# All sums of expert weights on VectorE, row weighting on ScalarE, and one copy ahead of a relu: gated linear attention feeding a mixture of experts

## The chip, the cores and the metric

The kernel runs on one core of a Trainium2 chip. The metric is device time in microseconds (us), median of several executions. One more execution is recorded by the hardware profiler; every row below comes from that one. Engines are named as in the profile: PE is TensorE's matmul side, PEld its weight loads, DVE is VectorE, ACT is ScalarE, POOL is GpSimd, SP is SyncE. A trailing q (PEq, ACTq) is that engine's sequencer.

## The reference, cut to what matters

Attention (4 batches, 8 heads, 768 steps, head size 48) gives 3072 tokens of 384 numbers. Each token then goes to one of 16 experts (4 groups of 4), whose result is scaled by the two gate weights:

```python
for g in range(G):
    xg = x[g_idx == g]
    ...
    for e in range(Eg):
        h = np.maximum(xg[mask_e] @ w1[g, e], 0.0)       # 384 -> 1024
        ye = h @ w2[g, e]                                # 1024 -> 384
        combined = g_w[mask_g][mask_e] * e_w[mask_e]
        out[tok_idx] = combined[:, None] * ye
```

All of it is float32.

## The kernel before, in words

Until about 128 us the attention runs and the tokens are sorted into slots by expert; the change touches nothing there. From then on experts are worked off one after the other, as "jobs". Job 0 is a small early piece, jobs 1 to 15 go through the function `seven`, and a last small job ends the kernel. Job j has 2m tokens (m falls from 108 to 84). The order of instructions on each engine is the order in which the program issues them; each engine works its own queue in order.

`seven` computes both layers with seven block products instead of eight, so it needs sums of weight blocks (s1 to s4, for each layer) and sums of token blocks (t1 to t5). On PE, one call of `add` or `sum_of` is a group of 16 matmul instructions. This text numbers them. First layer: G1 (a11 b11), G2 (a12 b21), G3 (a13 b31), G4 (s2 t2), G5 (s1 t1), G6 (s3 t3), G7 (a23 b32), G8 (s4 b22), G9 (a13 b32), G10 (a22 t4), G11 (a23 t5). Second layer: H1 (a11 c11), H2 (a12 c21), Z (32 instructions, the last third of the outputs), H3 (s2 t2), H4 (s1 t1), H5 (s3 t3), H6 (s4 c22), H7 (a22 t4). Each PSUM sum is built up over several groups, and partial sums are copied out between them by ACT: k1 after G1 (L1254), k2 after G4 (L1260), k5 after G5 (L1262), k3 after G7 (L1266). The same bank goes on being added to, so G6 has to wait until k2 is copied, G8 until k5 is, and G10 until k3 is.

DVE adds the copies up into the four quarters of the hidden layer: c11 (L1258), c22 (L1268), c12 (L1272); ACT puts the relu on each (L1239) and on c21, which comes straight from the bank of G11. Then DVE makes the token sums of the second layer (L1208 to L1211), turns the rows of the next job into columns (`columns`, L1342), makes its token sums (again L1208 to L1211, L1219), and adds up parts of the result (L1304, L1313, L1315). The last part of the result is an ACT copy (L1317).

The weight sums of one layer are four instructions on 128x512 numbers: s1, s2 on DVE (L1188, L1189) and s3, s4 on POOL (L1192, L1193). `work_between` says where in `seven` they are issued. In the kernel before, those of the next job's first layer are all issued at "third" (ahead of L1313 on DVE); those of its second layer on DVE at "fourth" (ahead of the destinations L1352, L1360 of that job) and on POOL at its "first".

The results of job j-1 are delivered at "first" of job j: DVE transposes them (L1327), DVE multiplies them with the tokens' weights (L1330), and POOL issues 6 or 7 indirect DMAs (L1334) that scatter the rows to the output. At "second", from job 2 on, one step of a small table for left-over tokens is made on DVE (`table_of_left_overs`, ten steps of different lengths).

Of the kernel before, what the change touches and what calls it, by code (L numbers as in the profile page):

```python
# [17 lines left out]
ALU = mybir.AluOpType  # L18
AF = mybir.ActivationFunctionType
# [4 lines left out]
P = 128  # L24
# [86 lines left out]
def gla_then_hierarchical_moe(  # L111
# [32 lines left out]
    nc = tc.nc  # L144
# [7 lines left out]
    DM = H * D  # L152
# [24 lines left out]
    QW = DM // 4 + 2  # L177
# [10 lines left out]
    def bank():  # L188
        return banks["of"].tile([P, 512], F32, name="bank")
# [991 lines left out]
    def weight_sums(a, first):  # L1181

        ws = mp.tile([P, 4, 512], F32, name="ws_1" if first else "ws_2")
        s1, s2, s3, s4 = (ws[:, i] if first else
                          ws[:, i].rearrange("p (f d) -> p f d", f=4) for i in range(4))

        def by_vector():
            nc.vector.tensor_tensor(out=s1, in0=a(1, 0), in1=a(1, 1), op=ALU.add)  # L1188
            nc.vector.tensor_tensor(out=s2, in0=s1, in1=a(0, 0), op=ALU.subtract)  # L1189

        def by_pool():
            nc.gpsimd.tensor_tensor(out=s3, in0=a(0, 0), in1=a(1, 0), op=ALU.subtract)  # L1192
            nc.gpsimd.tensor_tensor(out=s4, in0=a(0, 1), in1=s2, op=ALU.subtract)  # L1193

        return dict(of=(s1, s2, s3, s4), by_vector=by_vector, by_pool=by_pool)

    def first_sums(j):
        w1 = weights[j][0]
# [24 lines left out]
    def seven(job, w1, w2, xt, sums, tokens, between):  # L1223


        m = job["n"] // 2
        n = 2 * m
        V, A = nc.vector, nc.scalar
        hT = mp.tile([P, FC, CAP], F32, name="hT")
        quarter_of = [hT[:, 4 * i:4 * i + 4, k * m:k * m + m] for i in range(2) for k in range(2)]  # L1230
        c11, c12, c21, c22 = quarter_of
        kept = mp.tile([P, 4, 4, CAP // 2], F32, name="kept", bufs=1)
        k1, k2, k3, k5 = (kept[:, i, :, 0:m] for i in range(4))

        def four(z):
            return z[:, 0:4 * m].rearrange("p (f t) -> p f t", f=4)

        def relu_of(c, z=None):
            A.activation(out=c, in_=c if z is None else z, func=AF.Relu)  # L1239

        def add(z, w, x, start=False):
            for f in range(4):
                onto(z[:, f * m:(f + 1) * m], w[:, f * P:(f + 1) * P], x, start and f == 0)

        b11, b12, b21, b22 = (xt[:, dc, k * m:(k + 1) * m] for dc in range(2) for k in range(2))
        b31, b32 = (xt[:, 2, k * m:(k + 1) * m] for k in range(2))
        a11, a12, a13, a21, a22, a23 = (w1[:, dc, i * 512:(i + 1) * 512]
                                        for i in range(2) for dc in range(3))
        s1, s2, s3, s4 = sums[0]["of"]
        t1, t2, t3, t4, t5 = tokens  # L1250
        za, zb, zc = bank(), bank(), bank()

        add(za, a11, b11, True)
        A.copy(out=k1, in_=four(za))  # L1254
        add(zb, a12, b21, True)
        add(zb, a13, b31)
        between("first")
        V.tensor_tensor(out=c11, in0=k1, in1=four(zb), op=ALU.add)  # L1258
        add(za, s2, t2)
        A.copy(out=k2, in_=four(za))  # L1260
        add(zc, s1, t1, True)
        A.copy(out=k5, in_=four(zc))  # L1262
        add(za, s3, t3)
        add(za, a23, b32)
        relu_of(c11)
        A.copy(out=k3, in_=four(za))  # L1266
        between("second")
        V.tensor_tensor(out=c22, in0=k3, in1=k5, op=ALU.add)  # L1268
        add(zc, s4, b22)
        add(zc, a13, b32)  # L1270
        relu_of(c22)
        V.tensor_tensor(out=c12, in0=k2, in1=four(zc), op=ALU.add)  # L1272
        add(za, a22, t4)
        add(za, a23, t5)
        relu_of(c12)
        relu_of(c21, four(za))

        ts = mp.tile([P, 4, 4, CAP // 2], F32, name="ts_2", bufs=1)
        t1, t2, t3, t4 = (ts[:, i, :, 0:m] for i in range(4))
        token_sums(*quarter_of, t1, t2, t3, t4)  # L1280
        a11, a12, a21, a22 = (w2[:, 4 * k:4 * k + 4, i * P:(i + 1) * P]
                              for i in range(2) for k in range(2))
        s1, s2, s3, s4 = sums[1]["of"]
        yT = results[0]
        results.reverse()
        last = mp.tile([P, 4, CAP // 2], F32, name="kept_y", bufs=1)
        k1, k2, k3, k5 = (last[:, i, 0:m] for i in range(4))
        za, zb, zc, zd = (bank()[:, 0:w] for w in (m, m, m, n))

        def sum_of(z, w, x, start=False):  # L1290
            for f in range(4):
                onto(z, w[:, f], x[:, f], start and f == 0)

        sum_of(za, a11, c11, True)
        A.copy(out=k1, in_=za)
        sum_of(zb, a12, c21, True)
        between("weights")
        for f in range(FC):
            w = w2[:, f, 2 * P:3 * P]
            if job.get("whole"):  # L1300
                product(zd, w, hT[:, f, 0:n], n, f == 0, f == FC - 1)
            else:
                onto(zd, w, hT[:, f, 0:n], f == 0)
        V.tensor_tensor(out=yT[:, 0, 0:m], in0=k1, in1=zb, op=ALU.add)  # L1304
        between("third")
        A.copy(out=yT[:, 2, 0:n], in_=zd)
        sum_of(za, s2, t2)
        A.copy(out=k2, in_=za)
        sum_of(zc, s1, t1, True)
        A.copy(out=k5, in_=zc)  # L1310
        sum_of(za, s3, t3)
        A.copy(out=k3, in_=za)  # L1312
        V.tensor_tensor(out=yT[:, 1, m:n], in0=k3, in1=k5, op=ALU.add)  # L1313
        sum_of(zc, s4, c22)
        V.tensor_tensor(out=yT[:, 0, m:n], in0=k2, in1=zc, op=ALU.add)  # L1315
        sum_of(za, a22, t4)
        A.copy(out=yT[:, 1, 0:m], in_=za)  # L1317
        between("fourth")
        return yT
# [3 lines left out]
    def deliver_quarters(job, yT, dst):  # L1323

        nb, rows = job["nb"], job["rows"]
        yq = mp.tile([P, NB, DM // 4], F32, name="yq")
        nc.vector.transpose(  # L1327
            out=yq[:, 0:nb].rearrange("p b (c r) -> p b c r", c=DC),
            in_=yT[:, :, 0:32 * nb].rearrange("p c (b t) -> p b c t", t=32))
        nc.vector.tensor_tensor(  # L1330
            out=yq[:, 0:nb], in0=yq[:, 0:nb],
            in1=rows[:, 0:nb, QW - 2:QW - 1].to_broadcast([P, nb, DM // 4]), op=ALU.mult)
        for b in range(nb):
            nc.gpsimd.indirect_dma_start(  # L1334
                out=out_by.popleft().rearrange("n (j w) -> (n j) w", j=4),
                out_offset=bass.IndirectOffsetOnAxis(ap=dst[:, b:b + 1], axis=0),
                in_=yq[:, b, :], in_offset=None, bounds_check=4 * N - 1, oob_is_err=False)
# [131 lines left out]
    def deliver_last():  # L1469
        deliver_quarters(*pending.popleft())  # L1470
# [58 lines left out]
    xt = ahead["xt"]  # L1529
    sums = {1: [first_sums(1), second_sums(1)]}  # L1530
    tokens = {1: first_tokens(xt, ahead["n"] // 2)}
    for part in sums[1]:
        part["by_vector"]()
        part["by_pool"]()
    left_overs = table_of_left_overs()
    end = len(jobs) - 1
    turned = {1: xt}

    def work_between(j, what):
        job, after = jobs[j], jobs[j + 1]  # L1540
        if what == "first":
            if j > 1:
                sums[j][1]["by_pool"]()
            deliver_last()
        elif what == "second":
            if 1 < j:
                next(left_overs, None)
        elif what == "weights":
            if j + 2 < len(jobs):
                load_w1(j + 2, expert(jobs[j + 2]))  # L1550
        elif what == "third":
            if j == end - 1:
                n_left = nc.values_load(
                    table["n_more"][0:1, 0:1], min_val=0, max_val=NX,
                    skip_runtime_bounds_check_because="a count of at most NX")
                computed_left_over(n_left)
            turned[j + 1] = columns(after)
            if j + 1 < end:
                tokens[j + 1] = first_tokens(turned[j + 1], after["n"] // 2)
                sums[j + 1] = [first_sums(j + 1), second_sums(j + 1)]  # L1560
                sums[j + 1][0]["by_vector"]()
                sums[j + 1][0]["by_pool"]()
        elif what == "fourth":
            if j + 2 < len(jobs):
                load_w2(j + 2, expert(jobs[j + 2]))
            if j + 1 < end:
                sums[j + 1][1]["by_vector"]()

    jobs[end - 1]["whole"] = True
    for j, job in enumerate(jobs):  # L1570
        if j == 0:
# [84 lines left out]
```

## Time and profile before

| what | value |
|---|---|
| median of 3 runs | 420.25 us (415.59 to 421.2) |
| profiled execution, own time | 415.17 us |
| its span, first to last instruction | 413.2 us |
| mean granted TensorE clock | 0.977 |
| ACT busy in the span | 156.8 us |
| POOL busy in the span | 291.5 us |

The span is 2.0 us shorter than the execution's own time; steps below are made in the span and carried over one to one. The median lies 5.1 us above the profiled execution.

### The profile page before, as it was taken

How to read it: one execution, taken by the hardware profiler on the slowest of the kernel's cores; microseconds unless marked ns; L12 is line 12 of the kernel's file. 1: busy time of each engine (PE TensorE's matmuls, PEld its weight loads, DVE VectorE, ACT ScalarE, POOL GpSimd, SP SyncE). 2: the span in 40 equal slices, each digit the busy share in tenths (PEclk: the TensorE clock that was granted, in tenths of full speed). 3: DMA queues.
4: the chain of work that ended last, by engine and by line, in shares of the span. 5: the costliest groups of instructions: out<-in, count | busy, mean ns of one | idle time of the engine just before them, and what ended most of it. 6: DMA issues, size and time to landing. Idle time of an engine off the chain costs nothing. (4 is left out here: it accounts for less than half of the span.)

```text
span 413.2 us, 16779 instructions
## 1 busy us (share of the span) xinstructions
PE 369.2 (89%) x7098; PEld 339.5 (82%) x7098; DVE 335.3 (81%) x625; ACT 156.8 (38%) x430; POOL 291.5 (71%) x300
## 2 busy tenths in 40 slices
PE   7999999989899899898998888896998979779795
PEld 5888888868798798897988877796988979779794
DVE  7696999979677897887898789988889889788620
ACT  2767756755632223423232332323132332333220
POOL 7899599899764548585766767685766857667544
PEclk9999999999999999998999899997899999999898
DMA  8999998889868985666676555664677578547200
GB/s 299 393 398 376 390 372 275 291 276 367 300 239 255 235 302 194 199 221 182 233 250 221 184 186 183 189 221 156 203 264 251 184 214 295 199 172 245 101 24 31
DMA packets 32859, 98.87 MB, mean 239 GB/s; under 512 B 17957, under 2 KB 22179, under 8 KB 28432
## 3 DMA queue, kind: packets, MB, share of 16 engines
q1 hardware_dynamic: 26896, 87.14, 61.5%
q0 software_dynamic: 4832, 9.55, 6.6%
q8 instruction: 57, 0.93, 0.9%
q10 hardware_dynamic: 1056, 1.10, 0.9%
q14 instruction: 18, 0.15, 0.1%
HBM read 82.61 MB, written 15.60 MB: 238 GB/s over the span
## 5 line engine op out<-in xcount | busy, mean ns | idle before, releaser
L1334 POOL DMA_INDIRECT out_dram<-yq,dst_q x101 | 110.3, 1092 | 59.4 <-issue 26.1
L1178 PE MATMUL bank<-ts,ws 128*64 128x108 f32 (+14 forms) x1440 | 68.7, 248 | 1.0 <-PEq L1503 0.6
L1178 PE MATMUL bank<-hT,w 128*64 128x108 f32 (+28 forms) x928 | 65.9, 302 | 2.0 <-ACT hT L1239 2.0
L1178 PEld LDWEIGHTS bank<-ts,ws 128*64 128x64 f32 x1440 | 63.8, 137 | 4.3 <-issue 3.4
L1193 POOL TENSOR_TENSOR ws<-w,ws 128x512 f32<-128x512 f32 x30 | 38.9, 1296 | 35.6 <-DVE ws L1189 35.6
L1178 PE MATMUL bank<-ts,w 128*64 128x108 f32 (+14 forms) x720 | 39.3, 263 | 26.9 <-ACT kept L1266 26.9
L1178 PEld LDWEIGHTS bank<-hT,w 128*64 128x64 f32 x928 | 56.4, 149 | 7.9 <-ACT hT L1239 2.2
L1178 PEld LDWEIGHTS bank<-ts,w 128*64 128x64 f32 x720 | 34.4, 147 | 29.7 <-ACT kept L1266 29.7
L1178 PE MATMUL bank<-xt_e,w 128*64 128x106 f32 (+13 forms) x1120 | 54.8, 246 | 1.8 <-issue 1.8
L1178 PEld LDWEIGHTS bank<-xt_e,w 128*64 128x64 f32 x1120 | 50.0, 137 | 2.1 <-issue 1.9
L1313 DVE TENSOR_TENSOR yT<-kept_y 128x108 f32<-128x108 f32 (+14 forms) x15 | 38.9, 2593 | 12.4 <-ACT kept_y L1312 11.5
L1239 ACT ACTIVATE hT<-hT 128x432 f32<-128x432 f32 (+14 forms) x45 | 22.9, 529 | 62.1 <-DVE hT L1258 50.3
L1192 POOL TENSOR_TENSOR ws<-w 128x512 f32<-128x512 f32 x30 | 40.5, 1351 | 2.0 <-DMA slots_d<-xr,place 1.9
L459 DVE TENSOR_TENSOR_SCAN kd<-in,starts 112x516 f32<-112x516 f32 (+1 forms) x21 | 24.3, 1162 | 7.1 <-DMA in<-in_rows_dram 7.1
L736 POOL DMA_INDIRECT slots_d<-xr,place x24 | 24.1, 1004 | 6.3 <-issue 3.9
L475 POOL TENSOR_TENSOR in<-in,kd 112x512 f32<-112x512 f32 (+1 forms) x21 | 23.9, 1139 | 5.4 <-DVE kd L459 3.5
L582 PE MATMUL bank<-wr,yt 112*64 112x116 f32 x384 | 25.4, 267 | 1.5 <-ACT yt L574 1.5
L493 PE MATMUL zs<-in 48*64 48x128 f32 (+1 forms) x512 | 22.8, 276 | 3.6 <-POOL in L479 3.4
L479 POOL TENSOR_TENSOR in<-in,cq 112x512 f32<-112x512 f32 (+1 forms) x22 | 23.9, 1093 | 2.8 <-DVE cq L470 2.7
L470 DVE TENSOR_TENSOR_SCAN cq<-in,starts 112x516 f32<-112x516 f32 (+1 forms) x22 | 24.6, 1127 | 1.4
L1189 DVE TENSOR_TENSOR ws<-ws,w 128x512 f32<-128x512 f32 x30 | 24.6, 820 | 1.0
L1188 DVE TENSOR_TENSOR ws<-w 128x512 f32<-128x512 f32 x30 | 24.9, 829 | 0.0
(207 smaller groups left out, 689.2 us busy)
## 6 DMA issues: line engine op xcount, KB each, us to landing
w<-in_w_dram SPq DMA_DIRECT2D x34, 1536.0 KB, 7.3
in<-in_rows_dram SPq DMA_DIRECT2D x17, 962.5 KB, 10.0
slots_d<-blank SPq DMA_DIRECT2D x4, 1372.0 KB, 18.9
w<-in_rows_dram SPq DMA_DIRECT2D x4, 962.5 KB
xq<-slots_d SPq DMA_DIRECT2D x28, 85.8 KB, 5.7
xq<-slots_d SPq DMA_DIRECT2D x28, 73.5 KB, 6.3
out_dram<-yq,dst_q POOLq DMA_INDIRECT x101
in<-in_rows_dram SPq DMA_DIRECT2D x1, 704.0 KB
```

The source lines that it names most:

```text
L459: nc.vector.tensor_tensor_scan(out=flat(c.kd[:, p0:p1])[:, ::-1], data0=c.t[0:R, A1 * p1:A1 * p0:-1], data1=one_col.to_broadcast([R, A1 * ...
L470: nc.vector.tensor_tensor_scan(out=flat(c.cq[:, p0:p1]), data0=c.t[0:R, A1 * p0:A1 * p1], data1=starts[0:R, A1 * p0:A1 * p1], initial=1.0, ...
L475: nc.gpsimd.tensor_tensor(out=c.k[:, p0:p1], in0=c.k[:, p0:p1], in1=c.kd[:, p0:p1, 1:A1], op=ALU.mult)
L582: nc.tensor.matmul(z[s, p * W:(p + 1) * W], lhsT=c.yt[:, p, s], rhs=wr[:, p, :], start=True, stop=True)
L736: sent = nc.gpsimd.indirect_dma_start(out=slots_by[t], out_offset=bass.IndirectOffsetOnAxis(ap=m["place"][:, c:c + 1], axis=0), in_=xr[:, ...
L1178: nc.tensor.matmul(z[h], lhsT=w[:, h], rhs=x, start=start, stop=False, skip_group_check=True)
L1188: nc.vector.tensor_tensor(out=s1, in0=a(1, 0), in1=a(1, 1), op=ALU.add)
L1189: nc.vector.tensor_tensor(out=s2, in0=s1, in1=a(0, 0), op=ALU.subtract)
L1192: nc.gpsimd.tensor_tensor(out=s3, in0=a(0, 0), in1=a(1, 0), op=ALU.subtract)
L1193: nc.gpsimd.tensor_tensor(out=s4, in0=a(0, 1), in1=s2, op=ALU.subtract)
L1313: V.tensor_tensor(out=yT[:, 1, m:n], in0=k3, in1=k5, op=ALU.add)
L1334: nc.gpsimd.indirect_dma_start(out=out_by.popleft().rearrange("n (j w) -> (n j) w", j=4), out_offset=bass.IndirectOffsetOnAxis(ap=dst[:, b ...
```

## The change

The multiplication of the delivered rows goes from one DVE instruction to one ACT instruction for each of the 6 or 7 row blocks. s3 and s4 go from POOL to DVE, and POOL is left with the indirect DMAs alone. The places of issue change: at "third" only s1, s2 of the next job's first layer are issued; s3, s4 of it stand at "first", behind the transpose of the delivered rows and ahead of c11; all four sums of the second layer stand behind c11 at a new place, "sums", together with the step of the left-over table. Nothing of this is issued at "fourth" any more. The copy k3 is issued ahead of the relu of c11 instead of behind it.

```diff
-        def by_vector():
+        def two():
             nc.vector.tensor_tensor(out=s1, in0=a(1, 0), in1=a(1, 1), op=ALU.add)
             nc.vector.tensor_tensor(out=s2, in0=s1, in1=a(0, 0), op=ALU.subtract)
 
-        def by_pool():
-            nc.gpsimd.tensor_tensor(out=s3, in0=a(0, 0), in1=a(1, 0), op=ALU.subtract)
-            nc.gpsimd.tensor_tensor(out=s4, in0=a(0, 1), in1=s2, op=ALU.subtract)
-
-        return dict(of=(s1, s2, s3, s4), by_vector=by_vector, by_pool=by_pool)
+        def other_two():
+            nc.vector.tensor_tensor(out=s3, in0=a(0, 0), in1=a(1, 0), op=ALU.subtract)
+            nc.vector.tensor_tensor(out=s4, in0=a(0, 1), in1=s2, op=ALU.subtract)
+
+        return dict(of=(s1, s2, s3, s4), two=two, other_two=other_two)
...
         between("first")
         V.tensor_tensor(out=c11, in0=k1, in1=four(zb), op=ALU.add)
+        between("sums")
         add(za, s2, t2)
         A.copy(out=k2, in_=four(za))
         add(zc, s1, t1, True)
         A.copy(out=k5, in_=four(zc))
         add(za, s3, t3)
         add(za, a23, b32)
+        A.copy(out=k3, in_=four(za))
         relu_of(c11)
-        A.copy(out=k3, in_=four(za))
-        between("second")
         V.tensor_tensor(out=c22, in0=k3, in1=k5, op=ALU.add)
...
-        nc.vector.tensor_tensor(
-            out=yq[:, 0:nb], in0=yq[:, 0:nb],
-            in1=rows[:, 0:nb, QW - 2:QW - 1].to_broadcast([P, nb, DM // 4]), op=ALU.mult)
+        for b in range(nb):
+            nc.scalar.activation(out=yq[:, b, :], in_=yq[:, b, :], func=AF.Copy,
+                                 scale=rows[:, b, QW - 2:QW - 1])
...
-    for part in sums[1]:
-        part["by_vector"]()
-        part["by_pool"]()
+    sums[1][0]["two"]()
...
         if what == "first":
-            if j > 1:
-                sums[j][1]["by_pool"]()
             deliver_last()
-        elif what == "second":
+            sums[j][0]["other_two"]()
+        elif what == "sums":
+            sums[j][1]["two"]()
+            sums[j][1]["other_two"]()
             if 1 < j:
                 next(left_overs, None)
...
                 sums[j + 1] = [first_sums(j + 1), second_sums(j + 1)]
-                sums[j + 1][0]["by_vector"]()
-                sums[j + 1][0]["by_pool"]()
+                sums[j + 1][0]["two"]()
         elif what == "fourth":
             if j + 2 < len(jobs):
                 load_w2(j + 2, expert(jobs[j + 2]))
-            if j + 1 < end:
-                sums[j + 1][1]["by_vector"]()
```

## Rows read from the trace of the kernel before

**Rows 1.** The page, busy us (share of the span) and instructions by engine.

```profile
PE 369.2 (89%) x7098; PEld 339.5 (82%) x7098; DVE 335.3 (81%) x625; ACT 156.8 (38%) x430; POOL 291.5 (71%) x300
```

**Rows 2.** Waits of PE's weight loads, 128 to 395 us: total, times, longest.

```profile
PEld bank L1178 <- ACT kept L1266: 29.7, 15, 3.4
...
PEld bank L1178 <- ACT hT L1239: 2.2, 1, 2.2
```

**Rows 3.** Timeline of PE, one job (m = 99): start, length, what [idle before].

```profile
239.47 2.21 PE L1178 MATMUL bank<-xt_e,w 128*64 128x99 f32 x48
241.51 2.43 PE L1178 MATMUL bank<-ts,ws 128*64 128x99 f32 x48
243.74 0.88 PE L1178 MATMUL bank<-xt_e,w 128*64 128x99 f32 x16
...
245.12 0.88 PE L1178 MATMUL bank<-xt_e,w 128*64 128x99 f32 x16
247.82 1.58 PE L1178 MATMUL bank<-ts,w 128*64 128x99 f32 x32 [1.82 <-ACT kept L1266]
...
258.93 2.17 PE L1178 MATMUL bank<-xt_e,w 128*64 128x97 f32 x48
```

**Rows 4.** Timeline of ACT in the same job.

```profile
239.69 0.24 ACT L1317 COPY yT<-bank 128x100 f32<-128x100 f32 x1 [1.13 <-PE bank L1178]
240.42 0.49 ACT L1254 COPY kept<-bank 128x396 f32<-128x396 f32 x1 [0.49 <-PE bank L1178]
...
246.85 0.53 ACT L1239 ACTIVATE hT<-hT 128x396 f32<-128x396 f32 x1 [3.28 <-DVE hT L1258]
247.29 0.47 ACT L1266 COPY kept<-bank 128x396 f32<-128x396 f32 x1
```

**Rows 5.** Timeline of DVE in the same job.

```profile
238.59 3.21 DVE L1313 TENSOR_TENSOR yT<-kept_y 128x100 f32<-128x100 f32 x1 [1.54 <-ACT kept_y L1312]
...
241.89 0.68 DVE L1188 TENSOR_TENSOR ws<-w 128x512 f32<-128x512 f32 x1
...
243.47 1.20 DVE L1360 SCALAR_TENSOR_TENSOR dst_q<-xq,past_q 128x7 int32<-128x7 int32 x1
244.59 0.86 DVE L1327 STREAM_TRANSPOSE yq<-yT 128x672 f32<-128x672 f32 x1
245.49 0.86 DVE L1330 TENSOR_TENSOR yq<-yq,xq 128x672 f32<-128x672 f32 x1
246.26 0.56 DVE L1258 TENSOR_TENSOR hT<-kept,bank 128x396 f32<-128x396 f32 x1
246.74 0.53 DVE L1398 TENSOR_REDUCE whose<-past 128x23 f32<-128x368 f32 x1
```

**Rows 6.** Timeline of POOL at the same place.

```profile
240.38 1.29 POOL L1192 TENSOR_TENSOR ws<-w 128x512 f32<-128x512 f32 x1
243.37 1.27 POOL L1193 TENSOR_TENSOR ws<-w,ws 128x512 f32<-128x512 f32 x1 [1.71 <-DVE ws L1189]
```

**Rows 7.** One line each, all its instructions: duration ns min/median/max, first and last start.

```profile
L1313 DVE TENSOR_TENSOR yT<-kept_y x15: 245/3239/4428, 147.4 to 396.6; 128x108 f32<-128x108 f32 x1, 128x106 f32<-128x106 f32 x1, 128x105 f32<-128x105 f32 x1, 128x103 f32<-128x103 f32 x1
L1360 DVE SCALAR_TENSOR_TENSOR dst_q<-rows,past_q x1: 161/161/161, 128.7 to 128.7; 128x3 int32<-128x3 int32 x1
```

**Rows 8.** Windows: length, PE busy us (instructions), granted clock, DMA share, GB/s.

```profile
128.00:395.00 267.00, 234.79 (x4725) 0.97 0.65 213
284.00:296.00 12.00, 10.52 (x154) 0.72 0.44 157
```

**Rows 9.** ACT with a scale from SBUF: timeline of a pair, 60 us.

```profile
60.16 0.56 ACT L548 ACTIVATE state<-sums,kd 112x48 f32<-112x48 f32 x2
```

**Rows 10.** Timeline, a DVE token sum, the indirect DMA beside it, and another.

```profile
268.68 0.57 DVE L1208 TENSOR_TENSOR ts<-hT 128x388 f32<-128x388 f32 x1 [0.59 <-ACT hT L1239]
268.77 1.32 POOL L1334 DMA_INDIRECT out_dram<-yq,dst_q  x1 [0.30 <-issue]
...
273.35 0.97 POOL L1334 DMA_INDIRECT out_dram<-yq,dst_q  x1 [0.30 <-issue]
```

## The prediction, made before the change was run

> **What bounds the kernel now.** I read the shares of busy time first: PE 89%, DVE 81%, POOL 71% [rows 1]. PE is the fullest, but from 128 us on it doesn't run through: the table of waits gives 29.7 us to one edge, PE's weight loads waiting for the copy k3 (L1266), once in each of the 15 jobs, and 2.2 us to one wait for a relu [rows 2]. I take these from the weight loads and not from the matmuls, since a matmul's modelled end overlaps the next start: G9 and G10 start 2.70 us apart, groups otherwise 0.69, so the stop costs 2.01 where the row says 1.82 [rows 3].
>
> Why does k3 come late? The timeline of one job answers. G7 starts at 243.74 and lasts 0.88, so k3 could start at about 244.65; it starts at 247.29 because the relu of c11 stands ahead of it on ACT and begins only at 246.85, 3.28 us idle, released by the sum c11 (L1258) [rows 3, 4]. That sum is late because DVE works through L1313 (3.21 us for 100 columns), weight sums, L1360 (1.20 us for 7 numbers), the transpose and the weighting first [rows 5]. The two strange lengths lie exactly beside POOL's weight sums: L1313 ends at 241.80 where a sum on POOL ends at 241.67, L1360 at 244.67 where the next one ends at 244.64 [rows 6]. The same lines take 245 ns at their shortest, and 161 ns (on 3 numbers) where POOL runs no sum [rows 7]. So in this trace a two-input DVE instruction stands still while POOL's weight sum runs.
>
> The stops have a second price. From 128 us on the mean granted clock is 0.97 of the upper level, 2.4 GHz, and it falls in a few places only: around the longest stop (3.4 us [rows 2]) it is 0.72, part of the time at the lower level, 1.2 GHz. Busy time times the missing share is 234.8 x 0.03 = 7.0 us for the whole stretch and 10.5 x 0.28 = 2.9 in the worst window [rows 8].
>
> So the part that can be won is 29.7 + 2.2 + 7.0 = 38.9 us, and a PE-bound job of m = 99 takes 19.46 (239.47 to 258.93) less its two stops of 2.0 and 2.2, about 15.2 us [rows 2, 3].
>
> **The change, part by part**, as one job of m = 99 in times after its G1, at 239.47. PE's groups start at 0, 0.68, 1.36 (G1 to G3), 2.04, 2.78, 3.53 (G4 to G6), then 0.69 apart [rows 3].
>
> *DVE.* Off: the weighting, 0.86; the POOL stalls, 3.21 - 0.25 and 1.20 - 0.2. On: four sums at 0.68, 2.7 [rows 5, 7]. Net about -2 us a job. The load of a job is then two transposes 1.7, eight weight sums 5.4, three quarter sums 1.7, token sums 4 x 0.57 and 5 x 0.25, three result sums 0.75 and destinations 0.4, in all 13.5 us (the lengths not in rows 5 and 10 are those of the nearest width there). That is below 15.2, so DVE does not become the bound by its sum; its order has to be walked.
>
> The destinations are no longer held up and end before the last result copy does. L1317 ends at 239.93, 0.46 after G1 [rows 3, 4]. Transpose 0.49 to 1.36. s3, s4 take 1.35 and end at 2.71; G6 and G8 want them at 3.53 and 5.0, so this is hidden, with 1.4 us to spare at s3. c11 to 3.2. Four sums of the second layer, 2.65, to 5.85; H3 wants the first of them after 12 us. Then the table step x, then c22.
>
> *ACT.* k1 ends at 1.44 (240.91) [rows 3, 4]. The seven scalings wait for the transpose (1.36) and so start at about 1.44. No row shows this operation at this size. The nearest is the pair with a scale from SBUF on 48 columns: 0.56 us for two, single ones 0.33, so a step of 0.23 [rows 9]. For 96 columns I add what wider ACT copies add, (0.49 - 0.24)/(396 - 100) = 0.84 ns a column [rows 4], 0.04 us: step 0.27, single 0.37. The last ends at 1.44 + 6 x 0.27 + 0.37 = 3.43. k2, as long as k1 and before in time for G6, now ends at 3.43 + 0.49 less the 0.1 that the pair overlaps, 3.83. G6 starts at 3.85 instead of 3.53: a new stop of about 0.35 us a job, 15 x 0.35 = 5.2 us. Bounds: with the step of 0.23 and single 0.33 it is 0.1 a job (1.5 us); with no overlap, 7 x 0.37, k2 ends at 4.5 and it is 1.0 a job (15 us). I take the middle because the row shows the overlap. A job with six blocks has one scaling less, but also shorter groups; I count it alike.
>
> The Trainium skill speaks against this part: its page "ScalarE: Activation LUTs" (Rules for kernel authors) puts a plain multiply on VectorE. By that rule the weighting would stay where it was, 0.9 us ahead of s3. Worked through the rows, the 5.2 us at G6 would go, but c22 would come 0.9 later and every table step would count (9 us in place of the 3 below): about 387, which is no other result.
>
> *k3 ahead of the relu.* G7 now starts at 4.60 and ends at 5.48, k3 runs 5.5 to 5.97, G10 is due at 6.67: the stop of 29.7 us is gone. What is late next? c22 runs at 6.0, c12 when G9 is done (5.98 + 0.88), 6.87 to 7.42; its relu to 7.98; G11 ends at 8.24, the relu of c21 to 8.74. H1 ends 8.74, so H2 finds c21 just ready. Slack against DVE being late: c22 at 5.85 + x, c12, two relus behind it, c21 done at 7.95 + x, wanted at 8.75: x may be 0.8. Of the ten steps seven are shorter, two have two instructions as long as L1398, 1.1 us, and one has six, 3.3 us [rows 5]. Cost 0.3 + 0.3 + 2.5 = 3.1 us. The last of these stops is as long as those that lost the clock; half of what the worst window lost, 1.4 us [rows 8]. The rest of the job (token sums from 8.0, columns, next token sums, s1 and s2, done about 13.7) is ahead of L1313, which waits for H5 at about 14.7; the next job finds everything ready.
>
> *POOL* loses its 60 sums of about 1.3 us [rows 6] and starts its DMAs when the first scaling is done, at 1.8. Seven at 1.32 + 0.30 at most end by 13.2 [rows 10], before the job does, so it stays off the path. The weight loads on SP's queue are released by PE's last reads and by sums that now stand earlier in a job than H7; nothing on that queue moves back. Job 1 starts with two sums made instead of eight; its own walk is the same with three scalings. In the last job six scalings stand between two relus, hidden behind PE.
>
> **Sum**, against the profiled execution: 415.2 - 29.7 - 2.2 - 7.0 + 5.2 + 3.1 + 1.4 = 386.0 us. Against the median of the runs, 420.25, the difference is larger by 5; I read those 5 us as further clock or stop losses of other executions, which the changed kernel would lose in part too, and do not add them. A change within about 2% can't be told from none here.
>
> **Rivals.**
>
> *ACT's queue is the new bound.* The scalings cost their upper price and delay k2 by 1.0 us a job: 386 + 10 = 396, and up to 403 if the stops keep the 7.0 us of clock. For it: seven small instructions ahead of a copy that PE wants at once. Against: the pair's step.
>
> *DVE becomes the bound.* If L1313 and L1360 were long for a reason of their own, a job would need 13.5 + 3.0 + 1.0 = 17.5 us of DVE, against 267 / 15 = 17.8 now [rows 8]: 415 - 15 x 0.3, about 410. Against: the short instances [rows 7].
>
> *Slower: indirect DMAs stop DVE as the sums did.* The Trainium skill's page "SBUF — State Buffer" (SBUF: two separate sides) describes one port pair shared by GpSimd and VectorE as an exclusive lock held for a whole instruction, against DVE instructions with two SBUF inputs too. As a mechanism of this kernel: the DMAs of a job fall from 1.8 us on into the chain s3, s4, c11, four sums, c22. If each of seven stops DVE for the 0.97 us of an undisturbed one [rows 10], that is 6.8, less 0.8 of slack, 6.0 a job: 386 + 90 = 476. From 3.4 of seven on ((2.5 + 0.8) / 0.97) it is slower than before. Against it: a two-input token sum of 388 columns took 0.57 us right beside a DMA, and it was the DMA that stretched, to 1.32 [rows 10]. With the POOL sums the trace agrees with the rule, with the DMAs it doesn't.
>
> *It doesn't do what it says*: some other wait holds G10 anyway; near 415.
>
> **How the numbers follow.** Forecast 0.78, at 386; ACT bound 0.10, 396 to 403; DVE bound 0.06, 410; slower 0.04, 476; no effect 0.02. The range goes from 415.2 - 38.9 + 1.5 + 3.1 = 380.9, rounded down to 380, to the upper end of the ACT case, 403. Faster by over 2%: 0.78 + 0.10 + 0.02 = 0.90; within 2%: 0.06; slower: 0.04.
>
> **What would show it.** L1313 near 0.25 us and L1360 near 0.2 throughout; PE's waits for L1266 gone, and small ones for k2 (L1260) in their place; a granted clock near 1.00 from 128 us on; DVE near 300 us busy; scalings of about 0.37 us, 0.27 apart. I am wrong if PE waits for relus (L1239) at H2 in most jobs, if weight sums last over 0.7 us beside indirect DMAs, or if the clock falls in spite of short stops.

## The result, and the profile after

The changed kernel takes 388.92 us (median of 4 runs, 387.13 to 394.68) against 418.57 before (median of 4, 415.59 to 421.2). The ratio is 0.9279 with a 95% interval of 0.9179 to 0.9379, so 7.2% less. The ratio leaves out the execution of 394.68 us, which ran at a granted clock of 0.966. The profiled execution took 387.13 us, its span 385.4, its mean granted clock 0.992. The prediction was 386.

First the page, busy time by engine, the line that answers to [rows 1]:

```profile
PE 361.5 (94%) x7098; PEld 332.8 (86%) x7098; DVE 298.1 (77%) x669; ACT 183.2 (48%) x531; POOL 219.1 (57%) x240
```

PE does the same 7098 matmuls in 94% of a shorter span. VectorE, with 60 sums more (40 us), is 37 us less busy; the weighting that left it accounts for some 13 us, so about 65 us of standstills went. Next the waits of PE's weight loads, 120 to 380 us (total, times, longest), against [rows 2]:

```profile
PEld bank L1178 <- issue: 7.4, 7, 2.0
PEld bank L1178 <- ACT kept L1261: 5.3, 14, 0.5
PEld bank L1178 <- ACT hT L1239: 2.3, 1, 2.3
PEld bank L1178 <- ACT yT L302: 1.4, 1, 1.4
```

The 29.7 us for k3 (now L1266) have no row any more. In their place stand 5.3 us for k2 (L1261), a little in 14 of 15 jobs, and 2.3 us once, at H2. Both are in PE's timeline of the job m = 99 and the start of the next, to be read beside [rows 3]:

```profile
227.65 2.21 PE L1178 MATMUL bank<-xt_e,w 128*64 128x99 f32 x48
229.69 1.53 PE L1178 MATMUL bank<-ts,ws 128*64 128x99 f32 x32
231.47 0.90 PE L1178 MATMUL bank<-ts,ws 128*64 128x99 f32 x16 [0.24 <-ACT kept L1261]
...
234.25 1.53 PE L1178 MATMUL bank<-ts,w 128*64 128x99 f32 x32
235.61 0.85 PE L1178 MATMUL bank<-hT,w 128*64 128x99 f32 x16
238.56 5.26 PE L1178 MATMUL bank<-hT,w 128*64 128x99 f32 x48 [2.10 <-ACT hT L1239]
...
254.91 4.28 PE L1178 MATMUL bank<-hT,w 128*64 128x97 f32 x64
```

G4 and G5 are the 32 instructions at 229.69; G6 could follow 1.37 us later, at 231.06, and follows at 231.47: a stop of 0.41 from start to start. Counted from G1, as in the prediction, G6 starts at 3.82 us; it was 3.53 before. G10 at 234.25 follows G9 at once. In this job the longest table step stands ahead of c22, so H2 (the first 16 of the group at 238.56; Z is the other 32) comes late, and behind this stop H2 and Z run at a lower clock: 5.26 us for 48 instructions. The next job has no stop but the one at G6; its 64 instructions at 254.91 are H1's 16 with these 48 and take 4.28, so 3.6 without H1's 0.68 (half of the 1.36 from 234.25 to 235.61).

ACT in the same job, against [rows 4]:

```profile
228.60 0.49 ACT L1254 COPY kept<-bank 128x396 f32<-128x396 f32 x1 [0.49 <-PE bank L1178]
229.07 1.97 ACT L1331 ACTIVATE yq<-yq,xq 128x96 f32<-128x96 f32 x7
230.95 0.47 ACT L1261 COPY kept<-bank 128x396 f32<-128x396 f32 x1
...
233.10 0.49 ACT L1266 COPY kept<-bank 128x396 f32<-128x396 f32 x1 [1.30 <-PE bank L1178]
233.48 0.54 ACT L1239 ACTIVATE hT<-hT 128x396 f32<-128x396 f32 x1
237.10 1.02 ACT L1239 ACTIVATE hT<-hT 128x396 f32<-128x396 f32 x2 [3.08 <-DVE hT L1268]
```

Seven scalings take 1.97 us together and k2 follows on their heels; k3 now waits for PE (1.30), not PE for k3. The relus at 237.10 wait for c22 (L1268), behind the table step. Last the single lines of VectorE, against [rows 7] (durations in ns, min/median/max):

```profile
L1313 DVE TENSOR_TENSOR yT<-kept_y x15: 247/260/272, 146.6 to 368.9; 128x108 f32<-128x108 f32 x1, 128x106 f32<-128x106 f32 x1, 128x105 f32<-128x105 f32 x1, 128x103 f32<-128x103 f32 x1
L1360 DVE SCALAR_TENSOR_TENSOR dst_q<-xq,past_q x14: 166/167/169, 147.5 to 353.2; 128x7 int32<-128x7 int32 x7, 128x6 int32<-128x6 int32 x7
L1192 DVE TENSOR_TENSOR ws<-w x30: 648/665/686, 133.4 to 357.2; 128x512 f32<-128x512 f32 x30
```

The median of L1313 falls from 3239 to 260 ns, that of L1360 from 1200 to 167. The new sums take 0.67 us, though indirect DMAs run beside them.

### The profile page after: what moved, and what is told of

Same layout as the page of the kernel before. It is cut to its first block, busy times and chain, and to the rows that moved or that the text cites. A ratio compares the mean times of both kernels' runs of the same rounds, so it can differ in the third digit from the quotient of the medians.

```text
span 385.4 us, 16943 instructions
## 1 busy us (share of the span) xinstructions
PE 361.5 (94%) x7098; PEld 332.8 (86%) x7098; DVE 298.1 (77%) x669; ACT 183.2 (48%) x531; POOL 219.1 (57%) x240
## 5 line engine op out<-in xcount | busy, mean ns | idle before, releaser
L1334 POOL DMA_INDIRECT out_dram<-yq,dst_q x101 | 115.7, 1146 | 141.4 <-ACT yq L1331 97.4
L1178 PE MATMUL bank<-hT,w 128*64 128x108 f32 (+28 forms) x928 | 63.8, 293 | 2.1 <-ACT hT L1239 2.1
L1178 PEld LDWEIGHTS bank<-hT,w 128*64 128x64 f32 x928 | 53.1, 139 | 8.8 <-ACT hT L1239 2.3
L1178 PE MATMUL bank<-ts,w 128*64 128x108 f32 (+14 forms) x720 | 35.9, 247 | 3.4 <-issue 3.4
L1178 PEld LDWEIGHTS bank<-ts,w 128*64 128x64 f32 x720 | 32.1, 137 | 3.8 <-issue 3.8
L1306 ACT COPY yT<-bank 128x216 f32<-128x216 f32 (+14 forms) x15 | 4.8, 321 | 49.7 <-PE bank L1178 46.5
L1331 ACT ACTIVATE yq<-yq,xq 128x96 f32<-128x96 f32 x91 | 25.7, 362 | 0.0
L493 PEld LDWEIGHTS zs<-in 48*64 48x64 f32 (+1 forms) x512 | 18.7, 146 | 6.6 <-POOL in L479 5.6
L582 PEld LDWEIGHTS bank<-wr,yt 112*64 112x64 f32 x384 | 20.3, 137 | 2.1 <-ACT yt L574 1.6
L559 PE MATMUL zo<-sm,in 128*48 128x128 f32 (+1 forms) x320 | 22.0, 273 | 0.0
```

The source lines that it names most:

```text
L493: nc.tensor.matmul(c.zs[i][s, p, :], lhsT=c.k[r, p, s], rhs=c.q[r, p, :], start=True, stop=True)
L559: nc.tensor.matmul(of(c.zo, p)[o], lhsT=c.v[:, h * D:h * D + o.stop - o.start], rhs=c.sm[:, i, p, :], start=(p < 2), stop=(c.bc == 0), ski ...
L582: nc.tensor.matmul(z[s, p * W:(p + 1) * W], lhsT=c.yt[:, p, s], rhs=wr[:, p, :], start=True, stop=True)
L1178: nc.tensor.matmul(z[h], lhsT=w[:, h], rhs=x, start=start, stop=False, skip_group_check=True)
L1331: nc.scalar.activation(out=yq[:, b, :], in_=yq[:, b, :], func=AF.Copy, scale=rows[:, b, QW - 2:QW - 1])
L1334: nc.gpsimd.indirect_dma_start(out=out_by.popleft().rearrange("n (j w) -> (n j) w", j=4), out_offset=bass.IndirectOffsetOnAxis(ap=dst[:, b ...
```

## The experiments

They ran on three chips. On the first two the kernel before itself took 507 us, 21% more than above; on the third 417. So each kernel is compared with the runs of the kernel before on its own chip, and kernels with each other only where they ran on one chip.

**First chip (before: 507.44 us). Which part makes the gain?** The rival was my own part on k3: that its place on ScalarE is the cause.

e1, the kernel before with k3 alone moved:

```diff
-        relu_of(c11)
         A.copy(out=k3, in_=four(za))
+        relu_of(c11)
```

> The kernel before with one edit: the copy k3 ahead of the relu of c11. Theory L (VectorE is late because GpSimd's weight sums stop it; the order on ScalarE only decides at which group PE notices): the stop leaves G10 and comes back at H2, since c22 and c12 still stand behind c11 on VectorE. In the job of m = 91 c11 ends at 336.6, c12 would end near 338.0 and the relu of c21 near 339.0, and H2 would be due at 337.1: a stop of 2.0 against 2.4 before. About 0.5 us a job, 8 us in all: near 410, ratio 0.98, PE's waits of 20 us or more for relus (L1239). Rival O (the order on ScalarE is the cause, as the prediction's part on k3 has it): the 29.7 us go; 386 to 392, ratio 0.93.

Measured 496.56 us, ratio 0.9822 (0.9754 to 0.9889).

e2, the changed kernel with k3 alone moved back:

```diff
-        A.copy(out=k3, in_=four(za))
         relu_of(c11)
+        A.copy(out=k3, in_=four(za))
```

> The changed kernel with one edit undone: k3 again behind the relu of c11. Theory L: c11 now ends 3.2 us after G1 and its relu is done at 4.8, before k3's bank is full at 5.5, so the order no longer matters: within 1 us of the changed kernel, ratio 0.93, no wait for k3 at G10. Rival O: the stop at G10 returns with about 2 us a job; 412 to 418, ratio 0.99.

Measured 470.97 us, ratio 0.9269 (0.9208 to 0.933). PE's waits in this kernel (whole span, cut):

```profile
PE bank L1178 <- issue: 32.8, 92, 1.0
PE bank L1178 <- ACT kept L1261: 7.0, 13, 1.3
...
PE bank L1178 <- ACT kept L1267: 0.4, 2, 0.2
```

There is k2 (L1261); for k3 (L1267 here) only 0.4 us are left, in two jobs, though the relu of c11 is ahead of it again. The stops with no releaser also stand between G7 and G10 and can hide a late k3, so e4 is the cleaner test. The move of k3 is worth 1.8% alone; everything without it 7.3%. This speaks for theory L against O. The stops at H2 that I expected in e1, 20 us or more, are not to be seen as such: 3.5 us of waits for relus, but 45.3 us of stops with no releaser stand in the same groups, and hide them.

e3, the changed kernel with the weighting back on VectorE:

```diff
-        for b in range(nb):
-            nc.scalar.activation(out=yq[:, b, :], in_=yq[:, b, :], func=AF.Copy,
-                                 scale=rows[:, b, QW - 2:QW - 1])
+        nc.vector.tensor_tensor(
+            out=yq[:, 0:nb], in0=yq[:, 0:nb],
+            in1=rows[:, 0:nb, QW - 2:QW - 1].to_broadcast([P, nb, DM // 4]), op=ALU.mult)
```

> The changed kernel with the weighting back on VectorE (one instruction of 0.8 us behind the transpose). The stops for k2 at G6 (5.3 us) go, c22 comes 0.8 later, and each step of the left-over table costs its length (9 us in place of 4): 387 to 391, ratio 0.92 to 0.94. If ScalarE's scalings cost more than G6 shows, 382 or less. If VectorE is so full that 0.8 us a job come through whole, 389 + 12 - 5 = 396.

Measured 482.58 us, ratio 0.9521 (0.9465 to 0.9577): 12 us behind e2 on the same chip, a miss. The two differ in the place of k3 as well, so this is not the price of the weighting alone.

e4, the kernel before with s3 and s4 alone moved to VectorE:

```diff
-            nc.gpsimd.tensor_tensor(out=s3, in0=a(0, 0), in1=a(1, 0), op=ALU.subtract)
-            nc.gpsimd.tensor_tensor(out=s4, in0=a(0, 1), in1=s2, op=ALU.subtract)
+            nc.vector.tensor_tensor(out=s3, in0=a(0, 0), in1=a(1, 0), op=ALU.subtract)
+            nc.vector.tensor_tensor(out=s4, in0=a(0, 1), in1=s2, op=ALU.subtract)
```

> The kernel before with one edit: s3 and s4 on VectorE, each where it was issued; weighting on VectorE, k3 behind the relu. Theory L: VectorE is no longer stopped, c11 ends about 5.1 us after G1, its relu at 5.7, k3 at 6.2, in time for G10 at 6.3 (m = 99) or late by some tenths in the short jobs; the table steps have 0.5 us more slack: 380 to 390, ratio 0.91 to 0.93. Rival O: the stop at G10 stays near 2 us a job, 405 to 418.

Measured 501.35 us, ratio 0.9884 (0.9841 to 0.9927): a miss in time, while the mechanism shows. The two held-up lines, first in e1 (sums still on POOL), then in e4:

```profile
L1313 DVE TENSOR_TENSOR yT<-kept_y x15: 245/593/1121, 154.4 to 475.0; 128x108 f32<-128x108 f32 x1, 128x106 f32<-128x106 f32 x1, 128x105 f32<-128x105 f32 x1, 128x103 f32<-128x103 f32 x1
L1360 DVE SCALAR_TENSOR_TENSOR dst_q<-xq,past_q x14: 1193/1198/1211, 158.2 to 455.1; 128x7 int32<-128x7 int32 x7, 128x6 int32<-128x6 int32 x7
```

```profile
L1313 DVE TENSOR_TENSOR yT<-kept_y x15: 246/260/271, 158.6 to 483.2; 128x108 f32<-128x108 f32 x1, 128x106 f32<-128x106 f32 x1, 128x105 f32<-128x105 f32 x1, 128x103 f32<-128x103 f32 x1
L1360 DVE SCALAR_TENSOR_TENSOR dst_q<-xq,past_q x14: 166/166/169, 160.8 to 462.6; 128x7 int32<-128x7 int32 x7, 128x6 int32<-128x6 int32 x7
```

In e1 L1313 is held up less than in the first trace (median 593 ns against 3239): POOL's sum behind the DMAs often falls beside another instruction there, for instance beside a token sum (L1208, at 286.23 us) that takes 2.32 us in place of 0.57. Moving the sums to VectorE ends the standstills by itself, with the scatter in place. The stop for k3 is down to 1.7 us in one job, and in PE's timeline G10 follows G9 at once, 6.31 us after G1 (256.43), where it took 8.35 before [rows 3]:

```profile
262.05 0.86 PE L1178 MATMUL bank<-xt_e,w 128*64 128x100 f32 x16
262.74 0.75 PE L1178 MATMUL bank<-ts,w 128*64 128x100 f32 x8
263.82 0.42 PE L1178 MATMUL bank<-ts,w 128*64 128x100 f32 x4 [0.33 <-issue]
```

But from there on PE has stops for nothing that the profile shows, 47.5 us in all. These had to be understood first.

**Second chip (before: 506.77 us). Where do the unexplained stops come from?**

a2 is the changed kernel, unaltered (no diff).

> The changed kernel itself, unaltered, as the yardstick for the other kernels on this chip. If the chip is like the one of the prediction: near 388, ratio 0.93, stops for k2 at G6 of about 5 us. If PE's unexplained stops (issue) are many here too, they should stand where they stood in e1 to e4, between G7 and H2 of a job.

Measured 483.25 us, ratio 0.9511 (0.9432 to 0.9591). PE's stops with no releaser are 37.1 us here, and in the jobs looked at they stand between G7 and H2, as expected. The ratio is that of e3 (0.9521) and not that of e2 (0.9269), which lacks only the move of k3. So on chips like these two that move may cost 12 us; the two kernels did not run on one chip, and it is not shown.

e5, the changed kernel without the scatter in even jobs (those rows of the output are not written):

```diff
+    delivered = []
...
-        for b in range(nb):
+        delivered.append(1)
+        for b in range(nb if len(delivered) % 2 else 0):
             nc.gpsimd.indirect_dma_start(
```

> The changed kernel, but the indirect DMAs of the delivered rows are left out in every even job (those rows of the output are not written). It asks where PE's unexplained stops come from. Theory S (PE's supply of instructions is slowed while GpSimd issues indirect DMAs): the stops stand only in the odd jobs. Rival W (the 1.5 MB weight loads do it): they stand in odd and even jobs alike, since every job loads its weights. Rival V (VectorE or ScalarE work beside it): alike too. Time: lower than the changed kernel by about half of its issue stops under S, and the same under W and V.

Measured once, 441.1 us, 42 less than a2. The issue stops of the weight loads fell by half, from 56.4 to 28.9 us, as expected; the rest of the 42 us was not followed up. PE's timeline, cut: job 7 (odd, m = 99), job 8 (even, m = 97) and the first layer of job 9 (odd, m = 96):

```profile
262.50 0.43 PE L1178 MATMUL bank<-xt_e,w 128*64 128x99 f32 x5 [0.29 <-issue]
...
267.19 0.37 PE L1178 MATMUL bank<-ts,w 128*64 128x99 f32 x3 [0.35 <-issue]
267.92 0.43 PE L1178 MATMUL bank<-ts,w 128*64 128x99 f32 x5 [0.36 <-issue]
...
278.64 2.14 PE L1178 MATMUL bank<-xt_e,w 128*64 128x97 f32 x46
...
286.54 4.30 PE L1178 MATMUL bank<-hT,w 128*64 128x97 f32 x64
...
294.00 2.15 PE L1178 MATMUL bank<-xt_e,w 128*64 128x96 f32 x48
...
300.04 0.83 PE L1178 MATMUL bank<-xt_e,w 128*64 128x96 f32 x16
300.81 0.40 PE L1178 MATMUL bank<-ts,w 128*64 128x96 f32 x4
301.55 0.41 PE L1178 MATMUL bank<-ts,w 128*64 128x96 f32 x5 [0.34 <-issue]
```

and the indirect DMAs on POOL at that place (none between):

```profile
267.93 0.97 POOL L1337 DMA_INDIRECT out_dram<-yq,dst_q  x1 [0.30 <-issue]
296.06 1.34 POOL L1337 DMA_INDIRECT out_dram<-yq,dst_q  x1 [27.16 <-ACT yq L1333]
```

In odd jobs PE gets through four or five matmuls at a time, some 0.75 us apart; job 8 runs through, and takes 15.4 us from G1 to G1 where job 9 takes 21.3 (294.00 to 315.3). The granted clock falls as well, to 0.55 of the upper level from 306 to 308 us. ScalarE and VectorE are late too, at the same time. First k3 in job 7, which waits for G7 (done at 262.93), then c12 in job 9, which waits for G9 (done at 300.87):

```profile
265.69 0.49 ACT L1266 COPY kept<-bank 128x396 f32<-128x396 f32 x1 [2.63 <-remote]
```

```profile
305.35 0.55 DVE L1272 TENSOR_TENSOR hT<-kept,bank 128x384 f32<-128x384 f32 x1 [4.17 <-remote]
```

So on this chip the stops stand only in jobs that scatter: S against W and V. That it is the supply of instructions that suffers is argued, from three engines being late together, and not shown. Both late instructions wait for PE, so signals from PE that arrive late would fit them as well, a rival that was not tested. VectorE, while it has work, keeps its pace beside the DMAs: twelve instructions in job 7 follow each other without a stop from 258.59 to 265.67. On the chip of the first result the same scatter has no such stops.

e6, the scalings and the scatter behind k1 of the second layer, the table step moved and cut:

```diff
         if what == "first":
-            deliver_last()
+            sending.append(turned_rows(*pending.popleft()))      # the transpose
             sums[j][0]["other_two"]()
         elif what == "sums":
...
-            if 1 < j:
-                next(left_overs, None)
         elif what == "weights":
+            sending.pop()()                                      # scalings and indirect DMAs
...
                 sums[j + 1][0]["two"]()
+            if 1 < j < end - 1:
+                next(left_overs, None)
...
             nc.vector.tensor_reduce(out=total, in_=mine, axis=AX.X, op=ALU.add)
-        yield
+            yield
```

> The changed kernel with the scalings and the scatter issued behind k1 of the second layer, where ScalarE is idle for 3 to 5 us, instead of ahead of k2; the step of the left-over table behind the next job's s1, s2, and its longest step cut in two. If the two new stops are what the changed kernel still pays (G6 for k2, 5.3 us; H2 for the long step, 2.3 us and 1.7 us of clock), about 9 us less than the changed kernel, ratio 0.905 to 0.91 against the kernel before. If the stops only move on (to H5 for its k2, or to G4 for s2), no gain, ratio 0.93.

Measured 499.23 us, ratio 0.9839 (0.9776 to 0.9902): 16 us behind a2. The stops at G6 and H2 went, but a larger one came at H5 (weight loads' waits):

```profile
PEld bank L1178 <- ACT kept_y L1308: 43.5, 10, 5.9
PEld bank L1178 <- issue: 35.6, 32, 4.9
```

e4b is e4 again (no further diff), beside the changed kernel.

> The kernel of e4 again (before with s3 and s4 on VectorE where they were issued), next to the changed kernel on the same chip. In e4 the stop at G10 was down to 1.9 us, but 76 us of unexplained stops hid what that is worth. If those belong to the chip, then here the ratio is 0.91 to 0.94, near the changed kernel's. If they belong to the kernel, it stays near 0.99.

Measured 506.43 us, ratio 0.9932 (0.988 to 0.9984). On a chip with these stops the sums alone bring next to nothing, and the changed kernel 5%.

**Third chip (before: 417.34 us). The parts without the scatter.** All four kernels leave out the 101 indirect DMAs of the delivered rows, which stay unwritten:

```diff
-        for b in range(nb):
+        for b in range(0):
             nc.gpsimd.indirect_dma_start(
```

This chip turned out to be like that of the first result, so these compare with each other, and roughly with it. The kernel before was not run without the scatter, so what that alone brings is not known.

> The changed kernel without any of the 101 indirect DMAs that scatter the delivered rows (they are left out, the rows stay unwritten), so that the stops which some chips show beside them can't hide the rest. Under theory S the kernel then takes the same time on every chip: 388 less the 6 us of unexplained stops of the first trace, near 381, with stops for k2 at G6 of about 5 us and one of 2 us at H2. If it stays above 400, those chips are slow for another reason than the scatter.

Measured 386.06 us (385.97 to 386.57), ratio 0.9251 (0.9212 to 0.929). Five us above what I expected: without any scatter the waits of PE's weight loads (120 to 380 us) are

```profile
PEld bank L1178 <- issue: 7.0, 8, 2.0
PEld bank L1178 <- ACT kept L1261: 5.2, 14, 0.7
PEld bank L1178 <- ACT hT L1239: 2.2, 1, 2.2
```

The issue stops of such a chip are thus not the scatter's; the kernel before had 5.6 us of them too, in the same table.

The diff of e3 on top:

> The same without scatter, weighting on VectorE. By the prediction's sum the 5 us of G6 go and the table steps cost 9 in place of 4: equal to the kernel above within 2 us. If the 0.8 us a job on VectorE come through whole: 7 us more. If only the G6 stops count: 5 us less.

Measured 389.39 us (388.42 to 390.01), 3.3 us more than with the weighting on ScalarE, where 2 at most was expected. The stops changed their place:

```profile
PEld bank L1178 <- ACT hT L1239: 11.1, 13, 3.5
PEld bank L1178 <- issue: 3.5, 5, 2.0
```

That is my 5 us off at G6 against more at H2 for the table steps, 11.1 in place of the 9 of the prediction. In the profiled runs, 4.3 us apart, 2.0 of the difference lie ahead of G1 of job 1 (130.87 against 128.90), before the edit can act. From there to the end it is 257.4 against 255.1 us. The job with the longest table step alone takes 3.7 more (21.37 against 17.66 from G1 to G1, its mean granted clock 0.84 against 1.00); the others together gain.

The kernel of e4:

> The kernel before with s3 and s4 on VectorE in place (weighting on VectorE, k3 behind the relu), without scatter. Theory L: no stop for k2, c11 ends 5.1 us after G1, its relu at 5.7, k3 at 6.2 and G10 due at 6.3 to 5.4, so stops of 0 to 0.7 us at G10 in the short jobs and 1.8 for the long table step: within 5 us of the changed kernel without scatter, 374 to 384. Rival O (the place of k3 makes the gain): about 2 us a job at G10, 405 or more.

Measured 384.67 us (383.01 to 386.46), ratio 0.9228 (0.9175 to 0.9282), level with the whole change:

```profile
PEld bank L1178 <- issue: 7.8, 10, 1.9
PEld bank L1178 <- ACT kept L1266: 1.6, 2, 1.5
PEld bank L1178 <- ACT hT L1239: 1.6, 1, 1.6
```

With k3 still behind the relu and the weighting still on VectorE, the stop for k3 is down from 29.7 us to 1.6.

The kernel of e6:

> The kernel of e6 (scalings behind k1 of the second layer, table step moved and cut) without scatter. If the stops at G6 and H2 are all that is left beside the scatter, 9 us less than the changed kernel without scatter, near 372, with no wait for k2 (L1261) at G6 and none at H5 (L1308). If the scalings delay H5's k2 of themselves, no gain; then e6's 43 us of waits there were its own fault and not the scatter's.

Measured 382.88 us (381.5 to 386.15), ratio 0.9185 (0.9121 to 0.9249). The stops for k2 and at H2 are gone, and there is none at H5:

```profile
PEld bank L1178 <- issue: 7.1, 7, 2.0
...
PEld bank L1178 <- ACT hT L1239: 0.2, 1, 0.2
```

The gain is 3.2 us in place of 9, and hardly clear of the noise: one of the four executions took 386.15. In the profiled runs G1 of job 1 starts at 131.55 here and at 128.90 in the changed kernel without scatter; from there to the end it is 249.8 against 255.1 us, 5.3 less. What the late start has to do with the edit was not followed up. The 43.5 us at H5 of e6 were the scatter's on that chip, not the edit's own. Whether e6 beats the changed kernel with the scatter in place on a chip like the first was not run.

## Why the prediction was right

**What bounds the kernel: right.** PE from 128 us on, with VectorE's standstills beside POOL's sums as the cause. L1313 and L1360 fell to 0.26 and 0.17 us wherever the sums left POOL (a2, e2, e4), and L1360 stayed at 1.2 where they didn't (e1). The Trainium skill's page "SBUF — State Buffer" (SBUF: two separate sides) calls the port pair of GpSimd and VectorE an exclusive lock; the sums on POOL behaved so, with 1.2 us for an instruction of 0.17. For instructions with two SBUF inputs the page limits the lock to GpSimd operations that read SBUF, which the prediction left out when it set the DMAs against the rule.

**The size: right, the part it was put down to: not.** I wrote the 29.7 us down to the copy ahead of the relu. Alone (e1) it brings 1.8%, undone (e2) it leaves 0.4 us of waits for k3. With the sums alone moved the stop is 1.7 us (e4, scatter in place) or 1.6 (third chip) in place of 29.7. The reason was within reach: in my walk c11 ends 3.2 us after G1, so its relu is done (at 4.8, as worked out for e2) before k3 can start (5.5), and their order doesn't matter. I had the walk and did not draw that from it. The end of the stop is the sums' work. On the third chip, without the scatter, the three other edits add nothing that can be measured to it (386.06 against 384.67). What the sums alone are worth in time on such a chip with the scatter in place was not run.

**The new stop at G6: right.** Scalings of 0.36 us, 0.27 apart ((1.97 - 0.36) / 6), as estimated. G6 starts 3.82 us after G1, predicted 3.85, so 0.29 later than before; the prediction's own difference, 3.85 - 3.53, is 0.32, which it rounded to 0.35. PE's weight loads wait 5.3 us in all, predicted 5.2.

**The table steps and the clock: right within a microsecond.** One stop of 2.3 us at H2 and nothing from the two steps of 1.1 us, where I had 3.1 in all. H2 and Z behind it lost 5.26 - 3.6 = 1.7 us of clock, predicted 1.4. Around it the window shows the granted clock:

```profile
128.00:371.00 243.00, 230.80 (x4804) 0.99 0.72 235
238.00:244.00 6.00, 5.44 (x58) 0.72 0.59 237
```

With 0.99 in place of 0.97 over the stage [rows 8], 230.8 x 0.01 = 2.3 us are still lost of the 7.0, most of them here.

**VectorE's sum and POOL: right.** 298 us busy, predicted near 300.

**What is left.** Job 1 starts 1.6 us later (130.16 against 128.60, rows fetched later), and issue stops grew from 5.6 to 7.4 us; neither was in the sum. Against the profiled execution the sum missed by 1.1 us, against the median by 2.9. With the measured terms in it (clock 2.3, H2 2.3, G6 5.3, and these two) it would come to about 389.6, 2.5 us above the execution that they were read from. The clock, read in hundredths, may hide a part of that; a hit as close as 1.1 us is in part luck.

**The rivals.** ScalarE's queue did not take the upper price. VectorE did not become the bound: its long lengths were POOL's. Indirect DMAs do not stop VectorE: with seven a job beside them, the 30 s3 sums on VectorE took at most 0.69 us, and the DMAs themselves stretched, 1146 ns on average against 1092. The s2 sums (L1189) took up to 0.76, over the 0.7 that I had named as a sign of being wrong; the median of that line is 0.69. In e5 the scatter did slow PE, by 5 to 9 us a job, by a way that no rival had; the other chip of 507 us shows stops of the same kind beside the same DMAs. Of the chances, the case of no effect (near 415) belonged with "within 2%" and not with "faster", a slip of 0.02. The rule that I weighed against the trace, a multiply belongs on VectorE (the Trainium skill, "ScalarE: Activation LUTs", Rules for kernel authors), I put at 387, no other result. On the third chip the weighting on VectorE is 3.3 us slower by the medians and 2.3 by the profiled runs from G1 of job 1 on, so the trace speaks against the rule by very little.

## What to carry to other kernels

Before reading a long instruction as its own cost, look at what GpSimd does in the same microseconds: a 0.17 us instruction that takes 1.2 us wherever a sum runs on GpSimd is a wait, and moving such sums to the busier engine made it less busy. A stop put down to "A waits for B behind C" has two cures, B ahead of C or C earlier; walk both before saying which edit earns the gain. And an idle "issue" time that stands in the same jobs as another engine's DMAs is best tested inside one run, by leaving those DMAs out of every other job.

## What the runs showed that was not expected

Chips differ by 21% on the same program: 419 us for the kernel before in the first result and 417 on the third chip, 507 on two others. On the second chip each batch of indirect DMAs of 0.97 to 1.5 us makes a job 5 to 9 us longer; jobs without a batch run there as on the chip of the first result (m = 97: 15.4 us in e5, 15.3 in the trace of the result). It isn't the load on the DMA engines: in job 9 of e5 they are 0.10 to 0.17 busy from 302 to 306 us, while PE stops.

What differs in these chips is open. So is why the batch hurts more in e4b and e6, where it starts later in the job, than in a2 on the same chip, and what the 3.5 to 8 us of issue stops are that stay without any scatter.
